# First weights ahead of the second x tile, and block 0's scores regrouped into 18 full bursts

## The chip, the core and the metric

The kernel runs on one NeuronCore of one Trainium2 chip. Its five engines run their own instruction streams and meet at semaphores: TensorE (PE, with its weight loads shown as PEld), VectorE (DVE), ScalarE (ACT), GpSimd (POOL) and SyncE (SP), which here issues all the DMAs. The metric is the device time of one execution in microseconds (us), as the median of several runs. The time before is 702.66 us, the median of 4 runs between 700.46 and 703.07.

## The reference

One transformer block over 2048 tokens of width 1024: layer norm, attention with 32 heads of 32 and a causal window of 256, a residual, layer norm, a dense layer to 3584 with SiLU and back, a residual. All inputs are bf16.

```python
def _A_ref(x, wqkv, wo):
    H = 32; Dh = 32; W = 256
    q, k, v = split_heads(x @ wqkv)
    scores = einsum("bhqd,bhkd->bhqk", q, k) * Dh ** -0.5
    # key j is seen by query i where 0 <= i - j < W
    p = softmax(where(mask, scores, -1e9))
    return merge_heads(einsum("bhqk,bhkd->bhqd", p, v)) @ wo

h  = x + _A_ref(layernorm(x), wqkv, wo)
h2 = h + silu(layernorm(h) @ w1) @ w2
```

## The kernel before

**Tiling.** The tokens are cut into 4 blocks of 512, a block into 4 tiles of 128. The heads form 8 groups of 4: a group's 4 x 32 channels fill the 128 partitions, so that its four heads sit in four row groups of TensorE's array, and four matmuls of 32 rows each run there side by side. With tiles of 128 keys and a window of 256, a query tile sees its own key tile (masked above the diagonal), the one before it (no mask) and the one two before (masked the other way). A *chunk* below is one key tile against one query tile, 128 columns, for four heads. A head group of a block has 12 chunks; in block 0, where nothing comes before the first token, it has 9.

**Order of the work.** The order on each engine is the order in which the code emits it; a block's projections are computed while the block before goes through attention.

1. *Start-up.* SP issues, in this order, x tile 0, x tile 1, the first half of the V weights (`load_wqkv(2 * D)`, 1 MB), the second half, x tiles 2 and 3, then four 1 MB pieces of the Q and K weights (L127, L131). TensorE runs 11 matmuls on zeros (L152). For each x tile, `ln_first` takes statistics on VectorE (L162, L163), the square root on ScalarE (L191), the reciprocal (L194) and the normalisation in two halves (L183) on VectorE; `turn_first` transposes it on TensorE (L202) and copies it out on ScalarE (L203). `v_group(0, j, c)` is one dense group: 8 accumulating matmuls of 512 columns (L222) and a copy (L224). TensorE's order is: transposes of tile 0, V group (0,0), transposes of tile 1, V groups (1,0) and (0,1), transposes of tile 2, and so on. While ScalarE takes tile 0's square root, VectorE does half of tile 1's statistics (L193); the argument `then` stands for that.
2. *Block 0's Q and K*: 16 dense groups (L230), copied out by ScalarE and VectorE in turn (L232).
3. *Block 0's attention beside block 1's projections*, then the same for blocks 1 and 2. For each of 8 head groups and each of three kinds A, B, C of score burst: the burst, one dense group of the next block (24 in all, copied out by VectorE), and a third of the value work of the head group before.
4. Attention of block 3 beside the output projection; then the dense layers, which take more than half of the time.

**A score burst** (`scores`, L267) fills two PSUM tiles `sc`, one for each pair of heads, with up to four chunks; neighbouring query tiles of one key tile go in one matmul, a *piece* of up to 384 columns, which is four matmuls, one for each head. Then ScalarE takes the exponential of each pair (L278) into one of 12 buffers `ebuf` in turn, and GpSimd sets the masked corners to zero (L293). The next burst may write `sc` when both exponentials are done. In block 0 the kinds hold 3, 2 and 4 chunks and their exponentials cover 768, 512 and 1024 elements of a partition.

**Value work** (`attn_out`, L303) multiplies the exponentials with V, which carries a column of ones, so that the sum comes along: 36 matmuls of 33 columns for a head group in block 0, in `o_ps`. VectorE divides (`attn_norm`, L314, L315), and SP sends a DMA transpose (L323) back into `qT`; it is put on the list `late`, which is emptied at the next burst. `steps` and `turns` are the next block's layer norm on VectorE and its DMA transposes, one of them after each dense group.

`acc` has two PSUM banks that the dense groups use in turn, `o_ps` two, `sc` four.

Of the kernel before, what the change touches and what calls it, by code (L numbers as in the profile page):

```python
# [9 lines left out]
F32 = mybir.dt.float32  # L10
I32 = mybir.dt.int32
ACT = mybir.ActivationFunctionType
ALU = mybir.AluOpType

P = 128
# [16 lines left out]
]  # L32
KINDS = "ABC"


@with_exitstack
def kernel(
# [10 lines left out]
    nc = tc.nc  # L48
# [3 lines left out]
    S, D = x2d.shape  # L52
# [73 lines left out]
    def load_x(b, j):  # L126
        nc.sync.dma_start(out=x_ring[(b % 2) * 4 + j], in_=x2d[(b * 4 + j) * P:(b * 4 + j + 1) * P, :])  # L127

    def load_wqkv(c0):
        dst = wqk[:, :, c0:c0 + 512] if c0 < 2 * D else wv[:, :, c0 - 2 * D:c0 - 2 * D + 512]  # L130
        nc.sync.dma_start(out=dst, in_=wqkv_v[:, :, c0:c0 + 512])  # L131

    load_x(0, 0)
    load_x(0, 1)
    load_wqkv(2 * D)
    load_wqkv(2 * D + 512)
    load_x(0, 2)
    load_x(0, 3)
# [13 lines left out]
        nc.tensor.matmul(sc[0][:, i % 2, :], lhsT=warm[:, 0, 0:P], rhs=warm[:, 0, :], start=True, stop=True)  # L152


    def ln_stats(xt, st, j, stats=None):
        first = 0
        if stats is None:
            stats = small.tile([P, 2, 6], F32, name="ln_st", tag="ln_st")
        else:
            first = 1  # L160
        for c in range(first, 2):
            nc.vector.bn_stats(out=stats[:, c, :], in_=xt[:, c * 512:(c + 1) * 512])  # L162
        nc.vector.bn_aggr(out=st[:, j, :], in_=stats[:])  # L163

# [21 lines left out]
    def ln_transpose(xt, dst, j):  # L186
        nc.sync.dma_start_transpose(out=dst[:, :, j * P:(j + 1) * P], in_=xt)

    def ln_first(xt, st, rs, j, stats=None, then=None):
        ln_stats(xt, st, j, stats)  # L190
        nc.scalar.activation(out=rs[:, j:j + 1], in_=st[:, j, 1:2], func=ACT.Sqrt, bias=eps[:], scale=1.0)  # L191
        if then is not None:
            nc.vector.bn_stats(out=then[0], in_=then[1])  # L193
        nc.vector.reciprocal(out=rs[:, j:j + 1], in_=rs[:, j:j + 1])  # L194
        for h in range(2):
            ln_norm(xt[:, h * 512:(h + 1) * 512], st, rs, j)
# [19 lines left out]
        acc_n[0] += 1  # L216
        return acc_banks[acc_n[0] % len(acc_banks)]

    def v_group(b, j, c, copy):
        acc = next_acc()  # L220
        for kt in range(KT):
            nc.tensor.matmul(acc, lhsT=lnT_b[b % 2][:, kt, j * P:(j + 1) * P], rhs=wv[:, kt, c * 512:(c + 1) * 512],  # L222
                             start=(kt == 0), stop=(kt == KT - 1))
        copy(out=v[:, b * 4 + j, c * 16:(c + 1) * 16, 0:DH], in_=acc.rearrange("p (h d) -> p h d", d=DH))  # L224

    def qk_group(b, which, g, copy):
        acc = next_acc()
        col0 = which * D + g * P
        for kt in range(KT):
            nc.tensor.matmul(acc, lhsT=wqk[:, kt, col0:col0 + P], rhs=lnT_b[b % 2][:, kt, :],  # L230
                             start=(kt == 0), stop=(kt == KT - 1))
        copy(out=(qT, kT)[which][b][:, g, :], in_=acc)  # L232
# [9 lines left out]
    def run_late():  # L242
        while late:
            late.pop(0)()
# [12 lines left out]
    def e_of(i, kind, pair):  # L257
        return ebuf[(i * 6 + KINDS.index(kind) * 2 + pair) % 12]

    def scores(b, g, kind):  # L260
        for kt, q0, nq, ch in PIECES[kind]:
            t = b * 4 + kt
            if t < 0:
                continue
            for hh in range(4):
                r0 = hh * DH
                nc.tensor.matmul(  # L267
                    sc[hh // 2][:, hh % 2, ch * P:(ch + nq) * P],
                    lhsT=kT[t // 4][r0:r0 + DH, g, (t % 4) * P:(t % 4 + 1) * P],
                    rhs=qT[b][r0:r0 + DH, g, q0 * P:(q0 + nq) * P],  # L270
                    start=True, stop=True, tile_position=(r0, 0),
                )
        lo, hi = 0, 512
        if b == 0:
            lo, hi = {"A": (0, 384), "B": (256, 512), "C": (0, 512)}[kind]
        for pair in range(2):
            e = e_of(b * G + g, kind, pair)
            nc.scalar.activation(out=e[:, :, lo:hi], in_=sc[pair][:, :, lo:hi], func=ACT.Exp, scale=scale)  # L278
            if kind == "A":
                mask(e, 0, 1, True)  # L280
                mask(e, 2, 1 if b == 0 else 2, False)
            elif kind == "B":
                if b > 0:
                    mask(e, 1, 1, False)
                mask(e, 2, 1, True)
            else:
                mask(e, 0, 2, True)
                mask(e, 3, 1, False)

    def mask(e, c0, n, upper):  # L290
        ap = e[:, :, c0 * P:(c0 + n) * P].rearrange("p h (c q) -> p h c q", q=P)
        sgn = 1 if upper else -1
        nc.gpsimd.affine_select(out=ap, in_=ap, pattern=[[0, 2], [0, n], [sgn, P]],  # L293
                                compare_op=ALU.is_ge if upper else ALU.is_gt,
                                fill=0.0, base=0, channel_multiplier=-sgn)

    def attn_out(b, g, first, last):
        i = b * G + g
        for n in range(first, last):
            pair, qt, hh = n // 8, n // 2 % 4, n % 2  # L300
            chunks = [x for x in CHUNKS[qt] if b * 4 + x[0] >= 0]
            for m, (kt, kind, ch) in enumerate(chunks):
                nc.tensor.matmul(  # L303
                    o_ps[pair][:, qt * 2 + hh, 0:VW],
                    lhsT=e_of(i, kind, pair)[:, hh, ch * P:(ch + 1) * P],
                    rhs=v[:, b * 4 + kt, g * 4 + pair * 2 + hh, :],
                    start=(m == 0), stop=(m == len(chunks) - 1),
                )
            if n % 8 == 7:
                attn_norm(i, pair)  # L310

    def attn_norm(i, pair):
        recip = small.tile([P, 8, 1], F32, name="recip", tag="recip")
        nc.vector.reciprocal(out=recip[:], in_=o_ps[pair][:, :, DH:VW])  # L314
        nc.vector.tensor_tensor(  # L315
            out=obuf[i % 3][:, :, pair * 64:(pair + 1) * 64].rearrange("p t (h d) -> p t h d", d=DH),
            in0=o_ps[pair][:, :, 0:DH].rearrange("p (t h) d -> p t h d", h=2),
            in1=recip[:].rearrange("p (t h) o -> p t h o", h=2).to_broadcast([P, 4, 2, DH]), op=ALU.mult,
        )

    def attn_transpose(b, g):
        i = b * G + g
        nc.sync.dma_start_transpose(out=qT[b][:, g, :].rearrange("p (t q) -> p t q", q=P),  # L323
                                    in_=obuf[i % 3].rearrange("p t d -> p (t d)"))
# [8 lines left out]


    st, rs = ln_tiles("a")
    stats1 = small.tile([P, 2, 6], F32, name="ln_st", tag="ln_st")
    ln_first(x_ring[0], st, rs, 0, then=(stats1[:, 0, :], x_ring[1][:, 0:512]))
    turn_first(x_ring[0], lnT_b[0], 0)
    ln_first(x_ring[1], st, rs, 1, stats=stats1)
    v_group(0, 0, 0, act)  # L340
    turn_first(x_ring[1], lnT_b[0], 1)
    ln_first(x_ring[2], st, rs, 2)
# [15 lines left out]
    def ln1_steps(b):  # L358
        st, rs = ln_tiles("a")
        xs = [x_ring[(b % 2) * 4 + j] for j in range(4)]  # L360
        steps = [lambda j=j: ln_stats(xs[j], st, j) for j in range(4)]
        steps += rstd_steps(st, rs)
        for j in range(4):
            steps.append(lambda j=j: ln_norm(xs[j], st, rs, j))
        return steps, [lambda j=j: ln_transpose(xs[j], lnT_b[b % 2], j) for j in range(4)]
# [22 lines left out]
        nc.sync.dma_start(out=w1[:, kt, :], in_=w1_v[:, kt, :])  # L388


    pending = []
    for b in range(1, NB):
        dense = [lambda j=j, c=c: v_group(b, j, c, dve) for j in range(4) for c in range(2)]
        dense += [lambda w=w, g=g: qk_group(b, w, g, dve) for g in range(G) for w in range(2)]
        if b + 1 < NB:
            for j in range(4):
                load_x(b + 1, j)
            steps, turns = ln1_steps(b + 1)
        else:
            steps, turns = [], []  # L400
            nc.sync.dma_start(out=wo[:, 0:4, :], in_=wo_v[:, 0:4, :])
            nc.sync.dma_start(out=wo[:, 4:8, :], in_=wo_v[:, 4:8, :])
            load_res(0)
            load_res(1)
        n = 0
        for g in range(G):
            for kind in KINDS:
                run_late()
                if b == NB - 1 and n in (4, 10, 14):
                    load_w1({4: 7, 10: 6, 14: 5}[n])  # L410
                scores(b - 1, g, kind)
                dense[n]()
                if pending:
                    pending.pop(0)()
                if steps and n >= 1 and n != 3:
                    steps.pop(0)()
                elif turns and n % 3 == 2:
                    turns.pop(0)()
                n += 1
            pending = tail_of(b - 1, g)  # L420
        assert not steps and not turns
# [136 lines left out]
```

The softmax here doesn't subtract the row's maximum and nothing guards it: scores larger than these inputs give would overflow.

## Time and profile before

| | |
|---|---|
| median of the runs before | 702.66 us |
| the profiled execution's own time | 702.43 us |
| its span, first to last instruction | 700.6 us |
| TensorE busy | 688.3 us (98%) |
| VectorE, ScalarE, GpSimd busy | 286.0, 259.7, 171.6 us |
| start of the first V group | 9.54 us |
| block 0's first score burst | 54.91 us |
| block 1's first score burst | 111.93 us |

The profile is one execution on the chip. A line of a timeline gives start, length, engine, line of the kernel, operation, output <- input with shapes, count of merged instructions, and in brackets how long the engine stood idle before it and what ended that. Matmuls are pipelined: one is still on its way while the next has begun, so that a length is longer than the distance between two starts, and the distance is what a matmul costs. A line of the groups gives busy time, the mean of one in ns, and idle time with what ended it. The share of busy time is a mean over the whole span; a stretch of it is read from the table of stretches.

### The profile page before, as it was taken

The page shows a single profiled execution, that of the slowest core. Times are in us where ns is not written, and L with a number is a line of the kernel's source. Part 1 is how long each engine was busy: PE and PEld are TensorE (multiplying, and loading weights), DVE is VectorE, ACT ScalarE, POOL GpSimd, SP SyncE. Part 2 cuts the span into 40 slices and gives each one's busy share as a digit, 9 for nine tenths or more (in the row PEclk, how much of TensorE's full clock was granted, in tenths as well). Part 3 has the DMA queues.
Part 4 walks back from the last instruction along what each step waited for, and adds up shares of the span by engine and source line. Part 5 has one row for each costly group of instructions (what it writes and reads, how often), then busy time and mean ns, then how long its engine had stood idle before and what let it go on. Part 6 is the DMA issues. An engine that isn't in the chain of part 4 may idle for free.

```text
span 700.6 us, 12171 instructions
## 1 busy us (share of the span) xinstructions
PE 688.3 (98%) x4970; PEld 335.7 (48%) x5059; DVE 286.0 (41%) x608; ACT 259.7 (37%) x335; POOL 171.6 (24%) x375
## 2 busy tenths in 40 slices
PE   7999999999999999999999999999999999999998
PEld 3444555555555555544444444444444444444445
DVE  5255645654344437643324324434133351233111
ACT  3416667777777777621320023300033200233000
POOL 1004656777777777700000000000000000000000
PEclk9999999999999999999999999999999999999999
DMA  8522123024530568982022410023200034100010
GB/s 285 195 46 76 34 52 98 17 47 94 180 119 19 167 214 276 248 266 97 31 76 91 105 46 1 0 68 91 75 9 0 4 95 97 46 1 0 31 38 22
DMA packets 75399, 60.55 MB, mean 86 GB/s; under 512 B 49232, under 2 KB 59472, under 8 KB 75344
## 3 DMA queue, kind: packets, MB, share of 16 engines
q1 hardware_dynamic: 75344, 59.78, 30.1%
q8 instruction: 39, 0.64, 0.4%
q14 instruction: 16, 0.13, 0.1%
HBM read 39.85 MB, written 8.39 MB: 69 GB/s over the span
## 4 chain that ended last, share of the span: by engine, by line
PE 97%; DMA 1%; issue 1%; ACT 0%; SPq 0%; DVE 0%
PE hacc L468 18%; PE hacc L505 17%; PE acc L230 16%; PE acc L505 10%; PE acc L468 9%; PE acc L222 8%; PE acc L249 7%; PE o_ps L303 5%; PE sc L267 4%; PE hacc L249 1%; DMA r_w<-in_A_wqkv_dram 1%; PE o_ps L202 0%; SPq L127 0%; ACT r_a L224 0%; ACT r_w L203 0%
## 5 line engine op out<-in xcount | busy, mean ns | idle before, releaser
L278 ACT ACTIVATE r_e<-sc 128x1024 bf16<-128x1024 f32 (+2 forms) x192 | 175.8, 967 | 66.1 <-PE sc L267 52.5
L293 POOL TENSOR_SCALAR_AFFINE_SELECT r_e<-r_e 128x256 bf16<-128x256 bf16 (+1 forms) x368 | 168.6, 487 | 124.7 <-ACT r_e L278 121.5
L505 PEld LDWEIGHTS <-r_a 128*128 128x128 bf16 x952 | 90.9, 98 | 103.0
L468 PEld LDWEIGHTS <-r_w 128*128 128x128 bf16 x896 | 87.3, 98 | 104.8
L505 PE MATMUL hacc<-r_a 128*128 128x512 bf16 (+2 forms) x605 | 121.9, 359 | 0.6
L468 PE MATMUL hacc<-r_e,r_w 128*128 128x512 bf16 x444 | 100.2, 379 | 0.6
L477 ACT ACTIVATE r_n<-hacc 128x512 f32<-128x512 f32 x30 | 17.9, 597 | 178.9 <-PE hacc L468 178.9
L230 PEld LDWEIGHTS <-r_w 128*128 128x128 bf16 x512 | 46.2, 98 | 58.6 <-issue 8.9
L505 PE MATMUL acc<-r_a 128*128 128x512 bf16 x328 | 73.6, 379 | 0.4
L232 DVE CAST r_a<-acc 128x512 bf16<-128x512 f32 x56 | 38.6, 690 | 81.3 <-PE acc L230 57.7
L303 PEld LDWEIGHTS <-r_e 128*128 128x128 bf16 x1440 | 50.3, 96 | 22.7
L230 PE MATMUL acc<-r_t,r_w 128*128 128x512 bf16 x240 | 60.0, 380 | 0.8
L230 PE MATMUL acc<-r_w 128*128 128x512 bf16 x246 | 57.7, 380 | 0.5
L303 PE MATMUL o_ps<-r_a,r_e 128*128 128x33 bf16 x1440 | 51.2, 178 | 0.0
L249 PE MATMUL acc<-r_o,r_a 128*128 128x512 bf16 x196 | 48.7, 380 | 0.6
L468 PE MATMUL acc<-r_e,r_w 128*128 128x512 bf16 x216 | 49.1, 379 | 0.0
L249 PEld LDWEIGHTS <-r_a 128*128 128x128 bf16 x256 | 23.1, 98 | 29.6 <-issue 5.1
L267 PE MATMUL sc<-r_a 32*128 32x128 bf16 (+2 forms) x704 | 37.2, 276 | 0.0
L520 DVE SCALAR_TENSOR_TENSOR r_t<-hacc,r_t 128x512 bf16<-128x512 f32 (+2 forms) x22 | 14.0, 635 | 56.4 <-PE hacc L505 56.4
L222 PE MATMUL acc<-r_w 128*128 128x512 bf16 x122 | 31.0, 395 | 3.7 <-DMA r_w<-in_A_wqkv_dram 2.7
L520 DVE SCALAR_TENSOR_TENSOR r_t<-acc,r_t 128x512 bf16<-128x512 f32 x12 | 8.3, 691 | 64.2 <-PE acc L505 59.7
L478 DVE SCALAR_TENSOR_TENSOR r_a<-r_n,hacc 128x512 bf16<-128x512 f32 x30 | 20.6, 687 | 33.1 <-ACT r_n L477 33.1
(66 smaller groups left out, 424.2 us busy)
## 6 DMA issues: line engine op xcount, KB each, us to landing
r_w<-in_B_w_dram SPq DMA_DIRECT2D x8, 896.0 KB, 5.2
r_a<-in_B_w_dram SPq DMA_DIRECT2D x7, 1024.0 KB, 7.9
r_w<-in_A_wqkv_dram SPq DMA_DIRECT2D x6, 1024.0 KB, 11.2
r_o<-in_A_x_dram SPq DMA_DIRECT2D x16, 256.0 KB, 3.6
h_dram<-r_t SPq DMA_DIRECT2D x16, 256.0 KB, 3.3
r_t<-h_dram SPq DMA_DIRECT2D x16, 256.0 KB, 2.8
out_dram<-r_t SPq DMA_DIRECT2D x31, 128.0 KB, 1.7
r_e<-h_dram SPq DMA_DIRECT2D x3, 1024.0 KB, 5.8
```

The lines of the kernel that those rows point to most:

```text
L222: nc.tensor.matmul(acc, lhsT=lnT_b[b % 2][:, kt, j * P:(j + 1) * P], rhs=wv[:, kt, c * 512:(c + 1) * 512], start=(kt == 0), stop=(kt == KT ...
L230: nc.tensor.matmul(acc, lhsT=wqk[:, kt, col0:col0 + P], rhs=lnT_b[b % 2][:, kt, :], start=(kt == 0), stop=(kt == KT - 1))
L232: copy(out=(qT, kT)[which][b][:, g, :], in_=acc)
L249: nc.tensor.matmul(acc, lhsT=qT[b][:, g, j * P:(j + 1) * P], rhs=wo[:, g, c * 512:(c + 1) * 512], start=(g == 0), stop=(g == G - 1))
L267: nc.tensor.matmul(sc[hh // 2][:, hh % 2, ch * P:(ch + nq) * P], lhsT=kT[t // 4][r0:r0 + DH, g, (t % 4) * P:(t % 4 + 1) * P], rhs=qT[b][r0 ...
L278: nc.scalar.activation(out=e[:, :, lo:hi], in_=sc[pair][:, :, lo:hi], func=ACT.Exp, scale=scale)
L293: nc.gpsimd.affine_select(out=ap, in_=ap, pattern=[[0, 2], [0, n], [sgn, P]], compare_op=ALU.is_ge if upper else ALU.is_gt, fill=0.0, base ...
L303: nc.tensor.matmul(o_ps[pair][:, qt * 2 + hh, 0:VW], lhsT=e_of(i, kind, pair)[:, hh, ch * P:(ch + 1) * P], rhs=v[:, b * 4 + kt, g * 4 + pa ...
L468: nc.tensor.matmul(acc, lhsT=w1[:, kt, ft * P:(ft + 1) * P], rhs=ln2T[b][:, kt, :], start=(kt == 0), stop=(kt == KT - 1))
L478: nc.vector.scalar_tensor_tensor(out=gT[:, ft, :], in0=th, scalar=1.0, in1=acc, op0=ALU.add, op1=ALU.mult)
L505: nc.tensor.matmul(acc[:, 0:c1 - c0], lhsT=gT[:, ft, j * P:(j + 1) * P], rhs=w2[ft // 4][:, ft % 4, c0:c1], start=(ft == 0), stop=(ft == F ...
L520: nc.vector.scalar_tensor_tensor(out=t_out[j % 2][:, c0:c1], in0=acc[:, 0:c1 - c0], scalar=0.5, in1=t_in[j % 2][:, c0:c1], op0=ALU.mult, o ...
```

## The change

Two things are changed.

**Loads.** On SP's queue the first half of the V weights is issued behind x tile 0 and ahead of x tile 1. With it goes the early half of tile 1's statistics (`stats`, `then`): tile 1 now has its layer norm done as the others have.

**Block 0's attention.** The 72 chunks of its 8 head groups are put in one row (`first_stream`) and cut into 18 bursts of four. A burst may hold chunks of two head groups; it is made of one to three pieces. Its exponential always covers 1024 elements, and each masked chunk has a mask instruction of its own. The bursts are no longer tied to dense groups: `v_group` and `qk_group` call `between` ahead of each of their matmuls, and a burst is put in whenever 192/18 dense matmuls have passed, in the middle of a dense group where it falls so. The value work of a head group (`attn_out_first`) is cut into two units of 18 matmuls, one for each pair of heads; one unit follows a burst, from the burst after the group's last chunk on. What the last group leaves goes to the first dense groups of the next stage. Blocks 1 to 3 keep their loop, without the branches for block 0.

```diff
+def first_stream(n_groups):
+    bursts, where = [], {}
+    for g in range(n_groups):
+        for kt, q in ((0, 0), (0, 1), (0, 2), (1, 1), (1, 2), (1, 3), (2, 2), (2, 3), (3, 3)):
+            if not bursts or len(bursts[-1]) == 4:
+                bursts.append([])
+            where[g, kt, q] = (len(bursts) - 1, len(bursts[-1]))
+            bursts[-1].append((g, kt, q))
+    return bursts, where
...
     load_x(0, 0)
+    load_wqkv(2 * D)
     load_x(0, 1)
-    load_wqkv(2 * D)
     load_wqkv(2 * D + 512)
...
-    def v_group(b, j, c, copy):
+    def v_group(b, j, c, copy, between=None):
         acc = next_acc()
         for kt in range(KT):
+            if between:
+                between()
             nc.tensor.matmul(acc, ...
...
+    def scores_first(n):
+        ch = 0
+        while ch < 4:
+            g, kt, q0 = first_bursts[n][ch]
+            nq = 1
+            while ch + nq < 4 and first_bursts[n][ch + nq] == (g, kt, q0 + nq):
+                nq += 1
+            for hh in range(4):
+                r0 = hh * DH
+                nc.tensor.matmul(
+                    sc[hh // 2][:, hh % 2, ch * P:(ch + nq) * P],
+                    lhsT=kT[0][r0:r0 + DH, g, kt * P:(kt + 1) * P],
+                    rhs=qT[0][r0:r0 + DH, g, q0 * P:(q0 + nq) * P],
+                    start=True, stop=True, tile_position=(r0, 0),
+                )
+            ch += nq
+        for pair in range(2):
+            e = ebuf[(2 * n + pair) % 12]
+            nc.scalar.activation(out=e, in_=sc[pair], func=ACT.Exp, scale=scale)
+            for ch, (g, kt, q) in enumerate(first_bursts[n]):
+                if kt != q - 1:
+                    mask(e, ch, 1, kt == q)
...
-    stats1 = small.tile([P, 2, 6], F32, name="ln_st", tag="ln_st")
-    ln_first(x_ring[0], st, rs, 0, then=(stats1[:, 0, :], x_ring[1][:, 0:512]))
+    ln_first(x_ring[0], st, rs, 0)
     turn_first(x_ring[0], lnT_b[0], 0)
-    ln_first(x_ring[1], st, rs, 1, stats=stats1)
+    ln_first(x_ring[1], st, rs, 1)
...
+    def between():
+        k, m = count
+        if m * len(first_bursts) >= k * 192:
+            run_late()
+            scores_first(k)
+            if pending:
+                pending.pop(0)()
+            for g in range(G):
+                if first_where[g, 3, 3][0] == k:
+                    pending.extend([lambda g=g: attn_out_first(g, 0), lambda g=g: attn_out_first(g, 1)])
+            count[0] += 1
+        count[1] += 1
+
+    dense = [lambda j=j, c=c: v_group(1, j, c, dve, between) for j in range(4) for c in range(2)]
+    dense += [lambda w=w, g=g: qk_group(1, w, g, dve, between) for g in range(G) for w in range(2)]
+    for n in range(24):
+        dense[n]()
+        if steps and n >= 1 and n != 3:
+            steps.pop(0)()
+        elif turns and n % 3 == 2:
+            turns.pop(0)()
...
-    for b in range(1, NB):
+    for b in range(2, NB):
```

More of the change, by code (lines that the diff above doesn't have):

```diff
@@ L152, with ln_stats @@
         nc.tensor.matmul(sc[0][:, i % 2, :], lhsT=warm[:, 0, 0:P], rhs=warm[:, 0, :], start=True, stop=True)
[L155 to L161, printed above, removed]
+    def ln_stats(xt, st, j):
+        stats = small.tile([P, 2, 6], F32, name="ln_st", tag="ln_st")
+        for c in range(2):
             nc.vector.bn_stats(out=stats[:, c, :], in_=xt[:, c * 512:(c + 1) * 512])
@@ L187, in ln_transpose, with ln_first @@
         nc.sync.dma_start_transpose(out=dst[:, :, j * P:(j + 1) * P], in_=xt)
-    def ln_first(xt, st, rs, j, stats=None, then=None):
-        ln_stats(xt, st, j, stats)
+    def ln_first(xt, st, rs, j):
+        ln_stats(xt, st, j)
         nc.scalar.activation(out=rs[:, j:j + 1], in_=st[:, j, 1:2], func=ACT.Sqrt, bias=eps[:], scale=1.0)
-        if then is not None:
-            nc.vector.bn_stats(out=then[0], in_=then[1])
         nc.vector.reciprocal(out=rs[:, j:j + 1], in_=rs[:, j:j + 1])
@@ L224, in v_group, with qk_group @@
         copy(out=v[:, b * 4 + j, c * 16:(c + 1) * 16, 0:DH], in_=acc.rearrange("p (h d) -> p h d", d=DH))
-    def qk_group(b, which, g, copy):
+    def qk_group(b, which, g, copy, between=None):
         acc = next_acc()
@@ L229, in qk_group @@
         for kt in range(KT):
+            if between:
+                between()
             nc.tensor.matmul(acc, lhsT=wqk[:, kt, col0:col0 + P], rhs=lnT_b[b % 2][:, kt, :],
@@ L258, in e_of @@
         return ebuf[(i * 6 + KINDS.index(kind) * 2 + pair) % 12]
+    first_bursts, first_where = first_stream(G)
     def scores(b, g, kind):
@@ L262, in scores @@
             t = b * 4 + kt
-            if t < 0:
-                continue
             for hh in range(4):
@@ L272, in scores @@
                 )
-        lo, hi = 0, 512
-        if b == 0:
-            lo, hi = {"A": (0, 384), "B": (256, 512), "C": (0, 512)}[kind]
         for pair in range(2):
             e = e_of(b * G + g, kind, pair)
-            nc.scalar.activation(out=e[:, :, lo:hi], in_=sc[pair][:, :, lo:hi], func=ACT.Exp, scale=scale)
+            nc.scalar.activation(out=e, in_=sc[pair], func=ACT.Exp, scale=scale)
             if kind == "A":
                 mask(e, 0, 1, True)
-                mask(e, 2, 1 if b == 0 else 2, False)
+                mask(e, 2, 2, False)
             elif kind == "B":
-                if b > 0:
-                    mask(e, 1, 1, False)
+                mask(e, 1, 1, False)
                 mask(e, 2, 1, True)
@@ L288, in scores @@
                 mask(e, 3, 1, False)
+    def scores_first(n):
[16 more added lines that the diff above has]
+            e = ebuf[(2 * n + pair) % 12]
+            nc.scalar.activation(out=e, in_=sc[pair], func=ACT.Exp, scale=scale)
+            for ch, (g, kt, q) in enumerate(first_bursts[n]):
+                if kt != q - 1:
+                    mask(e, ch, 1, kt == q)
     def mask(e, c0, n, upper):
@@ L300, in attn_out @@
             pair, qt, hh = n // 8, n // 2 % 4, n % 2
-            chunks = [x for x in CHUNKS[qt] if b * 4 + x[0] >= 0]
-            for m, (kt, kind, ch) in enumerate(chunks):
+            for m, (kt, kind, ch) in enumerate(CHUNKS[qt]):
                 nc.tensor.matmul(
@@ L306, in attn_out @@
                     rhs=v[:, b * 4 + kt, g * 4 + pair * 2 + hh, :],
-                    start=(m == 0), stop=(m == len(chunks) - 1),
+                    start=(m == 0), stop=(m == 2),
                 )
@@ L310, in attn_out, with attn_out_first @@
                 attn_norm(i, pair)
+    def attn_out_first(g, pair):
+        for qt in range(4):
+            for hh in range(2):
+                kts = range(max(0, qt - 2), qt + 1)
+                for kt in kts:
+                    n, ch = first_where[g, kt, qt]
+                    nc.tensor.matmul(
+                        o_ps[pair][:, qt * 2 + hh, 0:VW],
+                        lhsT=ebuf[(2 * n + pair) % 12][:, hh, ch * P:(ch + 1) * P],
+                        rhs=v[:, kt, g * 4 + pair * 2 + hh, :],
+                        start=(kt == kts[0]), stop=(kt == qt),
+                    )
+        attn_norm(g, pair)
+        if pair == 1:
+            late.append(lambda: attn_transpose(0, g))
     def attn_norm(i, pair):
@@ L388, in load_w1 @@
         nc.sync.dma_start(out=w1[:, kt, :], in_=w1_v[:, kt, :])
+    for j in range(4):
+        load_x(2, j)
+    steps, turns = ln1_steps(2)
     pending = []
-    for b in range(1, NB):
+    count = [0, 0]
+    def between():
[18 more added lines that the diff above has]
+            turns.pop(0)()
+    assert not steps and not turns and count[0] == len(first_bursts)
+    for b in range(2, NB):
         dense = [lambda j=j, c=c: v_group(b, j, c, dve) for j in range(4) for c in range(2)]
```

## The prediction

> **What bounds the kernel now.** I read the shares of busy time first, then the chain that ended last, then the two stretches that the change touches.
>
> ```profile
> PE 688.3 (98%) x4970; PEld 335.7 (48%) x5059; DVE 286.0 (41%) x608; ACT 259.7 (37%) x335; POOL 171.6 (24%) x375
> ...
> PE 97%; DMA 1%; issue 1%; ACT 0%; SPq 0%; DVE 0%
> ```
>
> TensorE is the end-to-end limit: 97% of the chain is its own work. A microsecond taken out of its stream is a microsecond of the total, unless a wait comes back; work taken off ScalarE or GpSimd is worth nothing by itself. Next the start-up, in the timeline of TensorE and VectorE, and the clock in the stretch table (columns: stretch, its length, busy time and count of PE, PEld, DVE, ACT, POOL, clock, DMA share, GB/s):
>
> ```profile
> 6.21 0.63 PE L202 MATMUL o_ps<-ident,r_o 128*128 128x128 bf16 x8
> 9.54 3.50 PE L222 MATMUL acc<-r_w 128*128 128x512 bf16 x8 [2.70 <-DMA r_w<-in_A_wqkv_dram]
> 12.84 0.72 PE L202 MATMUL o_ps<-ident,r_o 128*128 128x128 bf16 x8
> 14.21 3.63 PE L222 MATMUL acc<-r_w 128*128 128x512 bf16 x15 [0.65 <-ACT r_w L203]
> ...
> 13.18 1.29 DVE L162 BATCH_NORM_STATS2 ln_st<-r_o 128x6 f32<-128x512 bf16 x2 [4.30 <-DMA r_o<-in_A_x_dram]
> 15.27 0.73 DVE L183 TENSOR_SCALAR r_o<-r_o,st_a,rs_a 128x512 bf16<-128x512 bf16 x2
> ...
> 9.54:12.84 3.30, 3.30 (x9) 1.12 (x9) 0.00 (x0) 0.00 (x0) 0.00 (x0) 0.52 1.08 362
> ```
>
> The first V group waits 2.70 us for its weights, which land at 9.50, and then runs at a granted clock of 0.52: 8 matmuls in 3.30, 0.41 each, against 15 in 3.63 (0.24) one group later. The second x tile has long been normalised by then (its last step ends at 8.88), so it is not what anybody waits for.
>
> Then one head group of block 0's attention, at 90 us:
>
> ```profile
> 89.87 0.52 PE L303 MATMUL o_ps<-r_a,r_e 128*128 128x33 bf16 x14
> 90.32 0.34 PE L267 MATMUL sc<-r_a 32*128 32x384 bf16 x4
> 90.59 1.90 PE L230 MATMUL acc<-r_t,r_w 128*128 128x512 bf16 x8
> 92.33 0.38 PE L303 MATMUL o_ps<-r_a,r_e 128*128 128x33 bf16 x9
> 92.64 0.29 PE L267 MATMUL sc<-r_a 32*128 32x256 bf16 x4
> 92.86 1.90 PE L230 MATMUL acc<-r_t,r_w 128*128 128x512 bf16 x7
> 94.60 0.48 PE L303 MATMUL o_ps<-r_a,r_e 128*128 128x33 bf16 x13
> 95.02 0.40 PE L267 MATMUL sc<-r_a 32*128 32x128 bf16 x8
> 95.34 1.90 PE L230 MATMUL acc<-r_t,r_w 128*128 128x512 bf16 x8
> ...
> 61.24 0.60 PE L267 MATMUL sc<-r_a 32*128 32x384 bf16 x4
> 61.77 1.90 PE L222 MATMUL acc<-r_w,r_t 128*128 128x512 bf16 x8
> ...
> 59.51 1.94 ACT L278 ACTIVATE r_e<-sc 128x1024 bf16<-128x1024 f32 x2 [1.08 <-PE sc L267]
> ```
>
> Read starts, not durations: matmuls overlap, so the cost of a burst is the time to the next line's start. Three score bursts cost 0.27, 0.22 and 0.32 for 384, 256 and 512 columns. That is 0.053 for each chunk of 128 columns and 0.11 on top, whatever the burst holds. Another 0.07 to 0.10 sits ahead of a burst: 14, 13 and 9 narrow value matmuls cost 0.45, 0.42 and 0.31, which is 0.025 each and about 0.09 left over, and with no value matmuls (57 us) a dense group needs 1.83 to the next burst against 1.74 to value matmuls. So a burst costs about 0.2 beyond its columns. Two bursts of three carry less than four chunks.
>
> **The change, part by part.**
>
> *Bursts.* The whole stretch is 57.02 (first burst at 54.91, block 1's first at 111.93). In it: 192 dense matmuls at 0.2157 (the spacing inside a group) 41.4; value matmuls of 7 groups, 252 at 0.025, 6.35; 72 chunks at 0.053, 3.84. Left: 5.4. One piece is visible as a wait: the burst at 61.24 costs 0.53 and not 0.27, since the exponentials of the burst before end at 61.45. The other 5.15 over 24 bursts is 0.215 each. After, 18 bursts cost 18 x 0.215 = 3.9: 1.3 less, and the 0.26 goes from this place, 1.5 in all.
>
> *Given back.* A burst that crosses head groups splits into more pieces: I count 42 pieces of 4 matmuls against 32, 40 more matmuls and weight loads, with six bursts of three pieces. Rows: a two-piece burst of 512 columns (95.02, 8 matmuls) costs 0.32, no more than the one-piece line 0.11 + 4 x 0.053. Here a rule speaks against the change: the Trainium skill, "TensorE: Matmul & The Clock Gate", section "Wait — 56ns, not 53.3ns?", says that starts never come closer than about 25 ns however small a matmul is. By the rule 40 more cost 1.0, and the six bursts of 12 matmuls 0.30 each against 0.21 of streaming, so the gain falls to 0.5. The value matmuls (one row group, 0.025 apart) agree with it; the four matmuls of a score piece, in four row groups, do not: the trace has them 3 ns apart, and 8 in 0.32 with 0.11 of switching. I follow the row and take 0.02 for each of the six third pieces, 0.1 (from 0 to 0.6).
>
> *The seam to block 1.* Left-over value work of the last group stays 36 matmuls, but in two units of 18 and not 9, 13 and 14. Block 1's third burst then has no value matmuls behind it: 0.42 + 1.74 = 2.16, while its exponentials need 0.43 (59.08 to 59.51) + 1.94 + 0.06 from burst start to release, 2.43. A wait of 0.27 appears there; one of 0.12 at 114.31 (that burst costs 0.45) goes. Cost 0.15.
>
> *The other engines in the stretch.* ScalarE: 36 exponentials of 1024 at 0.97 are 35 against 36.3 busy. Burst spacing is at least ten dense matmuls and a burst, 2.16 + 0.42 = 2.58, over the 2.43: no wait, with only 0.15 to spare. GpSimd: 96 masks of 128x256 against 64 of those and 16 of 128x512; at 0.42 and 0.64 that is 40 against 37, in 55.6: room. A burst's six masks take 2.5 of 2.58 at the closest. Value work of pair 0 comes one burst later (its first matmul about 3.0 after the burst start; its masks are done at 0.43 + 0.97 + 3 x 0.42 = 2.7), pair 1 two bursts later: covered, by 0.3 at the closest. If that cover goes, TensorE stands still behind the value matmul, and with it the dense group; the price is the shortfall, at up to 14 places. VectorE: dense groups may now follow at 1.73 instead of 2.05 to 2.45, while copy (0.69), a statistics step (1.5) and a normalisation (0.6) can ask 2.8. The two accumulators give a copy one whole group of slack, and laying copies and steps end to end from 57 to 73 us finds each bank free 1 us or more before it is asked for. SP: the same transposes and loads in the same order; the transpose of a head group is handed over at the next burst, and its reader is a stage away. Costed at nothing.
>
> Stage: 1.5 - 0.1 - 0.15 = 1.25; I take 1.15, from 0.5 (floor rule) to 1.5.
>
> *First loads.* On SP's queue the first V weights move ahead of the second x tile: issue 1.26 in place of 1.72, so 0.46 earlier at least. The queue also no longer moves 256 KB ahead of it; that took 0.65 (tile 0 lands at 3.4, tile 1 at 4.05 in the completion records). So the weights land at 8.85 to 9.05. Tile 1 comes behind them: a tile behind weights lands 0.7 later (second V weights 12.5, tile 2 13.2), so about 9.6. VectorE's statistics of tile 1, half of which was done in a gap at 4.91, are all ahead of it then: tile 2's row gives the pace, 13.18 to the first normalised half at 15.64, 2.46. Tile 1 can be transposed from 12.1. The V group, started at 8.95, needs 3.30 at the slow clock: 12.25. The transposes so move from 12.84 to about 12.25, 0.6 earlier, and what follows (ScalarE's copies, the next V groups) moves along: second V weights (12.5) and tiles 2 and 3 keep their place in the queue, and VectorE had tile 2 ready at 16.0 for transposes at 17.67, 1.6 to spare.
>
> Clock: the same page, section "What's actually happening", has the clock fall after an idle window of about 3.4. By that rule the gap of 2.70 would not slow the group, and a gap of 2.1 even less; the row says 0.52 after 2.70. By the row the group stays slow: gain 0.6. By the rule it ends at 10.7 and tile 1 decides, transposes at 12.1, with ScalarE free for their copies at once: gain about 0.9. I take the row and 0.65 with a little of the other.
>
> Sum: 1.15 + 0.65 = 1.8. The profiled execution has 702.43 (span 700.6 and 1.8 around it), 0.2 under the median 702.66: 702.66 - 1.8 = **700.8**, 0.26% down. About 0.3%, 2.1 us, is what a measurement of this kernel tells from no change.
>
> **Rivals.**
> - *The weights come much earlier.* In the completion records seven DMA engines have the first V weights by 7.5 and eight only by 9.5; between 4 and 6.4 the slow ones do nothing. If that gap belongs to the order (tile 1's small pieces ahead of the large), weights land by 8 and tile 1 by 8.7: transposes at 11.2, 1.65 gained; 1.15 + 1.65 = 2.8, so 699.9. Against it: nothing shows what the gap hangs on.
> - *The load order does nothing.* Weights still land at 9.5, tile 1 at 10.2, transposes at 12.85: only the stage, 701.5.
> - *Tile 1 becomes the bound, slower.* TensorE's queue holds tile 1's transposes behind the first V group, and behind them the next 16 V matmuls. Each us that tile 1 lands after 9.7 is a us there; if it lands as late as tile 2 (13.2), the transposes start at 15.7, 2.85 later, and after such a gap 16 V matmuls run part of a clock window (3.4) slow, up to 1.7 more. Minus 1.15: 703 to 706, 704.4 in the middle. It decides from a landing of about 11.5 (1.8 late, less 0.65 and 1.15). For it: the queue already spreads a transfer over 2.5 us. Against: per engine the landings keep the order of issue.
> - *Floor rule holds*: stage 0.5, 701.5, with the likely start-up.
>
> **How the numbers follow.** Likeliest case 0.57 (700.8; its own range 700.0 to 701.6), early weights 0.18, only one of the two parts pays 0.13, tile 1 late 0.12. Under 700.55 lie the early weights and 0.27 of the likeliest: faster 0.45. Slower is the late tile: 0.12. The rest, 0.43, is within 0.3%. The range leaves out half of the late-tile case and the best of the early-weights one: 699.0 to 703.0.
>
> **What would show it.** Right: the wait for the weights shrinks from 2.70 to about 2.1, the second set of transposes starts near 12.2, and from there to the first burst nothing changes; the first burst of block 1 comes 55.7 to 56 after block 0's first; no wait of TensorE on ScalarE or GpSimd inside. Wrong: a VectorE wait for the x tile past 10, a clock under 0.9 between 13 and 17 us, score bursts of three pieces over 0.4, value matmuls released by GpSimd, or dense matmuls released by a VectorE copy.

## The result and the profile after

The changed kernel takes 698.15 us (median of 32 runs, 697.96 to 701.6) against 702.2 for the kernel before (53 runs, 699.13 to 703.74); the ratio, of the means (698.5 and 701.7), is 0.9955, with a 95% interval of 0.9947 to 0.9963. That is 3.2 us (2.6 to 3.7) off, more than the 0.3% that can be told from no change, where 1.8 was forecast. The kernel before has two clusters of times: where each run's mean granted clock is known (88 of its runs, taken beside the experiments), 48 are at 0.999 or 1.000 with a median of 699.77, and 40 at 0.998 or less with 702.58; of the 53 runs above, 34 took 701.2 or more, as the second cluster does. The profiled run of before is of the second kind (0.998).

The profiled executions have spans of 700.6 and 696.5. First the start-up of the changed kernel, TensorE and VectorE, and the stretch table (columns as before: stretch, length, busy time and count of PE, PEld, DVE, ACT, POOL, clock, DMA share, GB/s):

```profile
6.22 1.06 PE L208 MATMUL o_ps<-ident,r_o 128*128 128x128 bf16 x8
7.53 1.91 PE L230 MATMUL acc<-r_w 128*128 128x512 bf16 x8 [0.25 <-ACT r_w L209]
10.13 0.72 PE L208 MATMUL o_ps<-ident,r_o 128*128 128x128 bf16 x8 [0.70 <-DVE r_o L191]
11.21 3.63 PE L230 MATMUL acc<-r_w 128*128 128x512 bf16 x15 [0.36 <-ACT r_w L209]
...
7.57 1.29 DVE L170 BATCH_NORM_STATS2 ln_st<-r_o 128x6 f32<-128x512 bf16 x2 [1.13 <-DMA r_o<-in_A_x_dram]
...
7.53:10.13 2.60, 1.90 (x8) 0.70 (x9) 2.13 (x6) 1.31 (x3) 0.00 (x0) 1.00 1.09 360
51.92:107.56 55.64, 54.89 (x603) 26.16 (x613) 34.53 (x80) 34.89 (x36) 37.06 (x94) 1.00 0.30 72
```

The wait of 2.70 for the weights is gone altogether: the first V group starts at 7.53 instead of 9.54 and waits only for ScalarE's copy of tile 0. It runs at full clock, 8 matmuls in 1.91. The second transposes now wait for VectorE, that is for x tile 1, whose layer norm begins when the tile lands (7.57), and start at 10.13 instead of 12.84. Block 0's first score burst is at 51.92 instead of 54.91: 2.99 from the start-up.

Then the bursts, and the seam to block 1:

```profile
60.13 0.40 PE L305 MATMUL sc<-r_a 32*128 32x384 bf16 x8
60.46 0.62 PE L346 MATMUL o_ps<-r_a,r_e 128*128 128x33 bf16 x18
...
63.40 0.40 PE L305 MATMUL sc<-r_a 32*128 32x128 bf16 x12
63.73 0.62 PE L346 MATMUL o_ps<-r_a,r_e 128*128 128x33 bf16 x18
...
107.56 0.40 PE L277 MATMUL sc<-r_a 32*128 32x384 bf16 x8
...
114.94 0.73 PE L277 MATMUL sc<-r_a 32*128 32x384 bf16 x8
115.61 1.90 PE L230 MATMUL acc<-r_w 128*128 128x512 bf16 x7
...
289.19 0.40 PE L277 MATMUL sc<-r_a 32*128 32x128 bf16 x8
```

and in the kernel before:

```profile
114.31 0.52 PE L267 MATMUL sc<-r_a 32*128 32x256 bf16 x8
114.76 1.90 PE L222 MATMUL acc<-r_w 128*128 128x512 bf16 x8
...
293.34 0.40 PE L267 MATMUL sc<-r_a 32*128 32x128 bf16 x8
```

A burst costs 0.33 from start to start, with 8 matmuls or with 12. The stretch is 55.64 where it was 57.02: 1.38 less. At the seam block 1's fourth burst, at 114.94, costs 0.67 instead of 0.33: the wait for the third burst's exponentials that was expected there. The wait of 0.12 in the kernel before (the burst at 114.31 costs 0.45) is gone. Block 3's last burst starts at 289.19 against 293.34, 4.15 earlier, which leaves 0.22 lost behind block 0: 2.99 + 1.38 - 0.22 = 4.15. These are two single executions; how much of the 2.99 holds for a typical run is what the experiments had to tell.

### The profile page after: what moved, and what is told of

It reads as the page before. It is cut to its first block, busy times and chain, and to the rows that moved or that the text cites. A ratio compares the mean times of both kernels' runs of the same rounds, so it can differ in the third digit from the quotient of the medians.

```text
span 696.5 us, 12252 instructions
## 1 busy us (share of the span) xinstructions
PE 686.1 (99%) x5012; PEld 332.4 (48%) x5099; DVE 287.8 (41%) x608; ACT 258.5 (37%) x323; POOL 174.5 (25%) x391
## 4 chain that ended last, share of the span: by engine, by line
PE 97%; DMA 1%; issue 1%; DVE 0%; ACT 0%; SPq 0%
PE hacc L540 18%; PE hacc L577 17%; PE acc L240 16%; PE acc L577 10%; PE acc L540 9%; PE acc L230 8%; PE acc L259 7%; PE o_ps L331 4%; PE sc L277 3%; PE hacc L259 1%; PE o_ps L346 1%; PE sc L305 1%; DMA r_o<-in_A_x_dram 1%; PE o_ps L208 0%; DVE ln_st L170 0%
## 5 line engine op out<-in xcount | busy, mean ns | idle before, releaser
L322 POOL TENSOR_SCALAR_AFFINE_SELECT r_e<-r_e 128x256 bf16<-128x256 bf16 (+1 forms) x384 | 171.6, 477 | 117.6 <-ACT r_e L314 66.2
L285 ACT ACTIVATE r_e<-sc 128x1024 bf16<-128x1024 f32 x144 | 139.5, 1021 | 45.1 <-PE sc L277 31.0
L240 PE MATMUL acc<-r_t,r_w 128*128 128x512 bf16 x241 | 58.5, 380 | 0.8
L240 PE MATMUL acc<-r_w 128*128 128x512 bf16 x246 | 57.7, 380 | 0.5
L331 PEld LDWEIGHTS <-r_e 128*128 128x128 bf16 x1152 | 39.6, 96 | 17.0
L314 ACT ACTIVATE r_e<-sc 128x1024 bf16<-128x1024 f32 x36 | 34.9, 1021 | 21.2 <-PE sc L305 20.1
L331 PE MATMUL o_ps<-r_a,r_e 128*128 128x33 bf16 x1152 | 40.2, 178 | 0.0
L540 PE MATMUL hacc<-r_a,r_w 128*128 128x512 bf16 x138 | 32.4, 379 | 0.3
```

The source lines that it names most:

```text
L285: nc.scalar.activation(out=e, in_=sc[pair], func=ACT.Exp, scale=scale)
L314: nc.scalar.activation(out=e, in_=sc[pair], func=ACT.Exp, scale=scale)
L331: nc.tensor.matmul(o_ps[pair][:, qt * 2 + hh, 0:VW], lhsT=e_of(i, kind, pair)[:, hh, ch * P:(ch + 1) * P], rhs=v[:, b * 4 + kt, g * 4 + pa ...
L540: nc.tensor.matmul(acc, lhsT=w1[:, kt, ft * P:(ft + 1) * P], rhs=ln2T[b][:, kt, :], start=(kt == 0), stop=(kt == KT - 1))
```

## The experiments

Two theories stood against each other. *Two parts*: the bursts give 1.1 in every run, and the new order of loads brings the weights far earlier, with the clock kept up besides. *Chance*: the profile of before had late weights by luck, and the order itself gives little.

**The load order alone**, in the kernel before:

```diff
     load_x(0, 0)
-    load_x(0, 1)
     load_wqkv(2 * D)
+    load_x(0, 1)
...
-    ln_first(x_ring[0], st, rs, 0, then=(stats1[:, 0, :], x_ring[1][:, 0:512]))
+    ln_first(x_ring[0], st, rs, 0)
...
-    ln_first(x_ring[1], st, rs, 1, stats=stats1)
+    ln_first(x_ring[1], st, rs, 1)
```

> The kernel before with the new load order alone (weights ahead of x tile 1, plain layer norm of tile 1), bursts as before. Theory (the order closes the gap in which half of the DMA engines stood still): first V group at about 7.5 us, second set of transposes at about 10.1, first score burst at 51.9, and 1.7 to 2.3 us off the median, some 60% or more of the whole gain; the attention stretch stays at 57.0. Rival (the late weights of the profile of before were chance, or the gain is in the bursts): first V group at 8.9 or later, under 1 us off.

Measured: 699.25 us in 12 runs, all at clock 1.000, ratio to before 0.9979 (0.9964 to 0.9993). TensorE in its profile:

```profile
7.26 1.90 PE L222 MATMUL acc<-r_w 128*128 128x512 bf16 x8 [0.35 <-ACT r_w L203]
9.84 0.72 PE L202 MATMUL o_ps<-ident,r_o 128*128 128x128 bf16 x8 [0.68 <-DVE r_o L183]
...
51.63 0.34 PE L267 MATMUL sc<-r_a 32*128 32x384 bf16 x4
...
108.64 0.40 PE L267 MATMUL sc<-r_a 32*128 32x384 bf16 x8
```

The start-up is that of the changed kernel, and the stretch between the last two lines is 57.01, as before. The order causes the early start. Its worth is 1.5 between the means and 0.85 between the medians, under the 1.7 to 2.3 that was expected: on this chip 22 of the 35 runs of before were at full clock. Against those alone (699.81) it is 0.56.

**The bursts alone**: the changed kernel with the two load lines and tile 1's early statistics put back.

```diff
     load_x(0, 0)
-    load_wqkv(2 * D)
     load_x(0, 1)
+    load_wqkv(2 * D)
...
-    ln_first(x_ring[1], st, rs, 1)
+    ln_first(x_ring[1], st, rs, 1, stats=stats1)
```

> The changed kernel with the old load order and the old handling of tile 1. Theory: the stretch from block 0's first burst to block 1's takes 55.6 as in the changed kernel, 0.2 to 0.3 come back at the seam, so about 1.1 us off; the first V group waits for its weights until 9.5 again, since the order sets that. Rival (chance): weights by 7.5 in this run too. Rival (bursts are the larger part): over 2 us off.

Measured: 701.7 us, ratio 1.0015 (1.0000 to 1.0030): the forecast of 1.1 off was missed. The stretch was as foretold, 55.69 to 111.33, 55.64. But 11 of the 12 runs had a clock of 0.998 or less, and in the profiled one the weights came later still, at 10.4:

```profile
10.41 3.40 PE L236 MATMUL acc<-r_w 128*128 128x512 bf16 x8 [3.04 <-DMA r_w<-in_A_wqkv_dram]
...
10.41:13.60 3.19, 3.19 (x8) 1.14 (x8) 0.00 (x0) 0.00 (x0) 0.00 (x0) 0.53 1.08 361
```

Among runs at 0.998 or less it has 701.93 against 702.75 for before, 0.8 off. Why the clock fell more often than in before (11 of 12 against 13 of 35), with the same start-up, stays open. The worth of the bursts comes from the first experiment: load order alone 699.25, both 698.15, so 1.1. These two medians are of different chips, between which the median of before at full clock differs by up to 0.45; the traces give 1.38 - 0.22 = 1.16 for the same.

**The clock alone.** In the trace of before the granted clock is at half for 3.41 us, just where the V group runs (same columns as above):

```profile
6.24:9.63 3.39, 0.69 (x10) 0.61 (x9) 1.85 (x6) 1.27 (x3) 0.00 (x0) 1.00 1.07 355
9.65:13.05 3.40, 3.40 (x10) 1.24 (x9) 0.00 (x0) 0.00 (x0) 0.00 (x0) 0.50 1.08 362
```

That stretch can cost at most 1.7 us, half of its length, and is the whole of that run's mean clock of 0.998 (0.5 x 3.41 / 700.6 = 0.24%). The next kernel is the one before with zeros multiplied while TensorE waits for the weights; the products are not used.

```diff
     ln_first(x_ring[1], st, rs, 1, stats=stats1)
+    for i in range(11):
+        nc.tensor.matmul(sc[0][:, i % 2, :], lhsT=warm[:, 0, 0:P], rhs=warm[:, 0, :], start=True, stop=True)
     v_group(0, 0, 0, act)
```

> The kernel before with 11 more matmuls on zeros between the transposes of tile 0 and the first V group, which fill TensorE's wait for the weights and compute nothing that is used. It measures what the slow clock alone is worth. Theory: weights still at 9.5, the group at full clock takes 1.73 instead of 3.30 and the second transposes start near 11.3 instead of 12.8: 1.0 to 1.5 us off in a run like the profiled one, and the spread of the run times shrinks[...]. Rival (the clock does not follow TensorE's idleness): group still at 0.41 a matmul, nothing gained.

Measured: 700.65 us, 12 runs from 700.17 to 701.81, all at 1.000; ratio 1.0002 (0.9987 to 1.0016). The runs above 702 are gone, and so are those at 699.5, since the 11 matmuls hold the V group until 9.09 although the weights were there at 8.5 in the profiled run. A shorter filler, the same with 8, was to take that objection away.

> The kernel before with 8 matmuls on zeros in TensorE's wait for the first V weights (they compute nothing that is used); the 11 of the first filler held the V group back to 9.09, these end by 8.5. Theory (the start-up's clock drop is a price of 2.5 to 2.7 us that some runs pay and some do not): all or nearly all runs at a mean clock of 1.000 and at 699.8 to 700.2, where the runs of before at full clock are, with the load order untouched. Rival (late weights cost the time, not the clock): half of the runs stay above 702.

Measured: 701.28 us (699.91 to 703.43), 11 of 12 runs at full clock, ratio 1.0004 (0.9988 to 1.0020). Its V group still starts at 9.94, at full clock:

```profile
6.68 1.89 PE L341 MATMUL sc<-r_e 128*128 128x512 bf16 x8
9.94 1.89 PE L222 MATMUL acc<-r_w 128*128 128x512 bf16 x8 [1.37 <-DMA r_w<-in_A_wqkv_dram]
11.66 0.61 PE L202 MATMUL o_ps<-ident,r_o 128*128 128x128 bf16 x8
```

The clock was held as foretold, but the time did not go to 699.8 to 700.2: the middle stayed at 701.2. So the 2.8 us between the two clusters of before (699.56 and 702.41 on that chip) are not the clock's alone, as the limit of 1.7 says too for a run at 0.998. Eight of the twelve runs lie at 701.2 to 703.4, where the profiled one (701.5) has its weights at 9.9. Read so, late weights cost about 1.7 with the clock held, and the clock about 1.2 more; the landing is known for the profiled run only, so this split is argued, not shown.

**The changed kernel again**, on another chip:

> The changed kernel, unaltered, beside the others of this call. Theory (two gains: 1.7 to 1.8 us at equal clock, and fewer runs whose clock drops in the start-up): nearly all runs at a mean granted clock of 1.000 and near 698.1; before splits into runs at 1.000 near 699.8 and runs under it near 702.7, so that the ratio depends on how many of each there are. Rival (one gain that is always there): before has one cluster, 3 us above.

Measured: 698.1 us, 7 runs from 698.0 to 698.84, none under 0.999; before 701.79 with 12 runs at full clock (700.02) and 18 at 0.998 or less (702.33); ratio 0.9956 (0.9940 to 0.9973). With the first batch, 3 of the 40 runs of the changed kernel whose clock is known have 0.998 or less, against 40 of 88 before.

**Why are the weights late in the old order?** Bursts as changed, old order, but the two x tiles in one transfer (shown against the old order):

```diff
-    load_x(0, 0)
-    load_x(0, 1)
+    nc.sync.dma_start(out=view(r_o, 0, 2, 1024), in_=x2d[0:2 * P, :].rearrange("(j p) d -> p j d", p=P))
     load_wqkv(2 * D)
```

> Bursts as changed, old order of loads, but x tiles 0 and 1 in one transfer of 512 KB ahead of the weights. It asks what makes some DMA engines late with the weights in the old order. If it is the second small transfer in front of them: all engines have the weights within 0.7 of each other, by 7.5. If it is the 512 KB in front, however issued: spread of 1.5 or more, weights at 8.5 to 10.5 as in the old order. Tile 0 comes 0.6 later in both.

Measured: 699.86 us, ratio 0.9978 (0.9962 to 0.9994). By the completion records of the profiled execution all DMA engines have the weights between 7.2 and 7.7, though 512 KB go ahead of them, as in the old order. In the four profiles with the two tiles apart the last engine has them at 9.5 (before), 10.4 (bursts alone), 8.5 and 9.9 (the two fillers), each time with the first at 7.0; in the changed kernel, its repeat and the four others that keep its order the spread is at most 0.65. This points away from the bytes ahead of the weights and to the second small transfer between them and the first. It is one execution, though, and of the quicker kind: 4 of the 10 runs are at 698.5, one at 699.96, and 5 at 699.8 to 700.7 with a clock of 0.998 or less, of which no profile was taken. Nor is a small transfer ahead enough by itself: in the changed kernel tile 1 stands straight ahead of the second half of the V weights, and these land within 0.7 of each other. What in the queue makes some engines late is not shown.

**What limits the start-up now.** The weights in two halves with tile 1 between, in the changed kernel:

```diff
-    load_wqkv(2 * D)
+    nc.sync.dma_start(out=wv[:, 0:4, 0:512], in_=wqkv_v[:, 0:4, 2 * D:2 * D + 512])
     load_x(0, 1)
+    nc.sync.dma_start(out=wv[:, 4:8, 0:512], in_=wqkv_v[:, 4:8, 2 * D:2 * D + 512])
```

> The changed kernel with the first V weights in two transfers of 512 KB, x tile 1 between them. Theory (tile 1 is now what the second set of transposes waits for): tile 1 lands 1.3 to 1.5 earlier, about 6.1; its layer norm ends by 8.6, the transposes follow the V group directly at about 9.3 to 9.5 in place of 10.1, 0.5 to 0.8 us under the changed kernel. Rival (the gap of the DMA engines comes back with a small transfer in front of a large one): weights at 8.5 or later, slower than the changed kernel by 1 us or more.

Measured: 698.68 us (698.23 to 700.42), ratio 0.9976 (0.9962 to 0.9989) beside a before of 700.1. Tile 1 came early and the transposes started at 9.44, as foretold:

```profile
7.23 1.04 PE L231 MATMUL acc<-r_w 128*128 128x512 bf16 x4 [0.35 <-ACT r_w L210]
8.58 1.02 PE L231 MATMUL acc<-r_w 128*128 128x512 bf16 x4 [0.31 <-DMA r_w<-in_A_wqkv_dram]
9.44 0.61 PE L209 MATMUL o_ps<-ident,r_o 128*128 128x128 bf16 x8
...
14.80 0.72 PE L209 MATMUL o_ps<-ident,r_o 128*128 128x128 bf16 x8 [0.40 <-DVE r_o L192]
```

But the late engines were back, from the piece behind tile 1 on: it lands over 1.6 us (6.9 to 8.5) and the second half of the V weights too (9.9 to 11.5), tile 2 at 12.2 instead of 11.2, and the third transposes wait for it. Its first burst is at 52.16. Half of each theory held; the sum is no gain.

The other way, tile 1 on ScalarE's own DMA queue, came together with a mend for the seam: the last group's value work in three units of 12.

```diff
-    load_x(0, 1)
+    nc.scalar.dma_start(out=x_ring[1], in_=x2d[P:2 * P, :])
...
+                    cuts = (0, 8, 16) if g < G - 1 else (0, 6, 12, 16)
```

> The changed kernel with x tile 1 issued from ScalarE's DMA queue at the start, so that it does not wait behind the weights, and the last head group's value work in three units of 12, which gives block 1's third burst its cover. Theory: tile 1 lands by 5, its transposes follow the V group at 9.1 to 9.4 in place of 10.1, and the wait of 0.27 at the third burst of block 1 goes: 0.7 to 1.1 us under the changed kernel. Rival (a second queue, or a small transfer beside the large one, brings back the late engines): weights at 8 or later, V group late, no gain or a loss.

Measured: 700.29 us in 12 runs, one of which (724.37 at a clock of 0.947) is left out of the ratio, 0.9979 (0.9963 to 0.9995). Of the other 11, 6 have a clock of 0.997 or 0.998, and 5 are at full clock with 698.79. With both tiles in flight tile 0 lands at 4.7 instead of 3.6, so that the first transposes start at 7.27 and the V group at 8.34. The weights are all there by 7.6, so the rival's late engines did not come back, yet the loss was larger than the gain: 0.7 to 1.1 better was expected. At the seam of the same run block 1's fourth burst went from 0.67 to 0.36; so this mend was run by itself:

> The changed kernel with the last head group's value work in three units of 12, nothing else. Theory: the wait of 0.27 at block 1's third burst goes as it did beside the other queue, 0.2 to 0.3 under the changed kernel, near 697.85. Rival: the wait moves to the next burst and the time stays.

```profile
114.31 0.46 PE L346 MATMUL o_ps<-r_a,r_e 128*128 128x33 bf16 x12
114.71 0.43 PE L277 MATMUL sc<-r_a 32*128 32x384 bf16 x8
115.07 1.90 PE L230 MATMUL acc<-r_w 128*128 128x512 bf16 x8
```

Measured: 697.87 us (697.75 to 698.02, 6 runs), ratio 0.9956 (0.9939 to 0.9972). From block 1's first burst to its fifth it takes 9.99 (107.29 to 117.28) instead of 10.25 (107.56 to 117.81), so the wait did not move on to the next burst. It has the lowest median here; the lead of 0.2 to 0.3 over the changed kernel fits these 0.26, but the two were timed on different chips.

**What a burst and a piece cost.** The changed kernel with 24 bursts of three chunks:

```diff
-            if not bursts or len(bursts[-1]) == 4:
+            if not bursts or len(bursts[-1]) == 3:
...
-        while ch < 4:
+        while ch < 3:
...
-            nc.scalar.activation(out=e, in_=sc[pair], func=ACT.Exp, scale=scale)
+            nc.scalar.activation(out=e[:, :, 0:384], in_=sc[pair][:, :, 0:384], func=ACT.Exp, scale=scale)
```

> The changed kernel with the stream of chunks cut into 24 bursts of three in place of 18 of four; exponentials of 768 elements, 32 pieces as in the kernel before, all else as changed. Theory (a burst costs 0.2 whatever it holds): the stretch goes from 55.64 to 56.8 or 56.9, six times 0.2 more, and 1.0 to 1.3 us are added to the changed kernel. Rival (the gain is in the even spacing of bursts inside the dense groups, or in ScalarE's shorter list): stretch under 56.1.

Measured: 699.59 us (699.46 to 699.96), ratio 0.9979 (0.9968 to 0.9991), 1.5 above the changed kernel on the same chip. The stretch:

```profile
51.78:108.70 56.92, 56.39 (x563) 25.67 (x573) 33.48 (x80) 36.28 (x48) 36.55 (x95) 1.00 0.26 51
```

Against 55.64 that is 1.28 for six bursts, 0.21 each, and the kernel before, whose 24 bursts stand between dense groups, has 57.02. So the number of bursts is the cause; their place inside dense groups, with the rest of the new loop, makes 0.1. And with one piece for each chunk (288 score matmuls instead of 168):

```diff
-            while ch + nq < 4 and first_bursts[n][ch + nq] == (g, kt, q0 + nq):
+            while ch + nq < 0:
```

> The changed kernel with every chunk as a piece of its own: 72 pieces, 288 score matmuls of 128 columns in place of 168, same columns. Theory (four row groups side by side, a piece costs its columns): a burst stays at 0.33 to 0.36, the stretch grows by 0 to 0.5. Rival (floor of 25 ns for a matmul): 16 matmuls cost 0.40 and the switch 0.11, 0.51 for a burst, the stretch grows by 3.2 to 59.

Measured: 698.38 us, ratio 0.9957 (0.9943 to 0.9972), 0.28 above the changed kernel on that chip; the stretch from 51.67 to 107.40 is 55.73.

```profile
59.90 0.40 PE L305 MATMUL sc<-r_a 32*128 32x128 bf16 x16
60.23 0.62 PE L346 MATMUL o_ps<-r_a,r_e 128*128 128x33 bf16 x18
```

Sixteen matmuls cost the 0.33 that eight do.

## Why the prediction was right, and where not

**The stage: right, each term within about 0.1.** Forecast 1.5 from six bursts and the freed wait, less 0.1 for pieces and 0.15 at the seam, 1.15 taken. Measured: 1.38 in the stretch, 0.22 back at the seam, 1.1 between the load order alone and both. The price of 0.215 for a burst was measured as 0.21. The third pieces cost nothing (0.33 and 0.33), less than the 0.1 allowed; the floor rule, which would have left 0.5, does not hold for these matmuls in four row groups: 16 of them and the switch take 0.33, where 16 at 25 ns are 0.40 already. The covers held: no wait of TensorE on VectorE's copies, and on GpSimd only 0.4 us of weight loads.

**The start-up: the direction right, the size not.** The step that failed is "so the weights land at 8.85 to 9.05". It moved the landing by the queue's own figures, 0.46 of issue and 0.65 of bytes, and left the late engines as they were. They did not stay: the weights land at 6.8 in the changed kernel's profile, so that the term priced at 0.65 is 2.99 in that pair of executions. That is the rival "the weights come much earlier", given 0.18, and even it was too careful (transposes at 11.2; measured 10.13). The profile showed the hint, seven engines early and eight late, with 180 to 230 GB/s from 4.6 to 5.9 us where 350 and more is usual; the prediction named it and could not say what it hung on. It hangs on the order of the loads, as the load order alone shows (V group at 7.26); that it is the second small transfer ahead of the weights rests on the one profile with the tiles merged and on the split weights.

**The clock: a row taken for a constant.** The prediction took the row's 0.52 and reckoned the V group at 3.30 after as well as before. It had one execution; the clock's fall comes in 40 of 88 runs of before and 3 of 40 after. By the rule weighed there, a gap of 2.70 leaves the clock alone; runs of both kinds exist, so neither row nor rule was the whole of it, and what decides in a given run stays open. In the profiled pair this is 1.6 of the V group's time (3.30 against 8 x 0.2157). At full clock in both, the change is worth 699.77 - 698.13 = 1.6. That this is near the 1.8 forecast is luck: the forecast was reckoned for an execution with late weights and a low clock, and for that one the pair of profiles shows 4.15. The rest of the 3.2 is that late weights and low clock, together 2.8 us, have become rare.

**Rivals.** Tile 1 did become what the second transposes wait for (0.70 at 10.13), but it lands at 7.55, not beyond 11.5, and so never costs what it saves. "The load order does nothing" fell with the first experiment. The median 698.15 lies under the low end of the range, 699.0, which was drawn from a median of 702.66; 0.9955 of that is 699.5, inside it.

## What to carry to other kernels

Where TensorE is full, count its switches between row-tiled and full matmuls: here each trip costs 0.2 us whatever it carries, so fill each burst, and do not fear small pieces inside one. In a start-up, look at how far apart the DMA engines finish one transfer, not only at when the last byte lands: with a second small load in front of the large one, the last engine was 1.5 to 3.3 us behind the first in four profiles here, and in the one profile with the same bytes in one load 0.5. And ask of a time from one profile whether it is a constant or a draw, above all for the clock after an idle gap.

## What the runs showed that was not expected

- Two tiles of 256 KB ahead of 1 MB leave single engines up to 3.3 us behind the first ones (7.0 to 10.4), differently in each profile; with the tiles merged it was 0.5, in one profile.
- A transfer on a second queue was not free: tile 0, with tile 1 issued at the same moment on the other queue, landed at 4.7 instead of 3.6.
- The clock is kept and lost by the same program: in 48 and in 40 of 88 runs of before.
